# Filter halves on two load queues, a sign moved into a product, and a shifted schedule, in an FFT-mixing plus swish-MLP kernel

## The chip, the cores and the metric

The kernel runs on one core of a Trainium2 chip. The metric is the device time of one execution in microseconds (us). TensorE (PE in the profile) multiplies, VectorE (DVE), ScalarE (ACT) and GpSimd (POOL) do the rest, and loads are issued by SyncE (SP) and by GpSimd; they then run on 16 DMA engines.

## The reference, cut to what matters

```python
# x (8, 3008, 256); filt_r, filt_i (1505, 256); w_in (256, 2048); w_out (2048, 256)
X = np.fft.rfft(x, axis=1)
y = np.fft.irfft(X * (filt_r + 1j * filt_i), n=3008, axis=1)   # per batch and channel
h = y.reshape(24064, 256) @ w_in
out = (h / (1 + exp(-beta * h))) @ w_out
```

The transform of length 3008 = 47 x 64 is done in two stages as matrix products (s1 and s2 forward, s3 and s4 inverse). The filter is applied between s2 and s3.

## The kernel before

The program has two parts. The **setup** loads the filters and weights, builds the DFT tables and transforms batch 0, since no MLP can run before a batch is mixed. The **main loop** has 752 steps; each does one slice of the MLP (`hps`, silu to `gT`, `acc`), and a plan places pieces of the later batches' transforms between them.

```python
# setup: filters, 128 partitions; the upper 64 hold the same values as the lower 64
def load_filter(f_sb, filt, ks, ds):
    lo = AP(...)   # rows k0.. , 32 partitions
    hi = AP(...)   # mirrored rows, 32 partitions
    for p0, src in ((0, lo), (M, lo), (H, hi), (M + H, hi)):      # M = 64, H = 32
        nc.sync.dma_start(f_sb[p0 : p0 + H, ks, ds], src)
# called six times: fr, fi for the first 8 k; fr, fi for the rest, twice (two column halves)
...
def s2_0(n):                       # six units for batch 0
    ... matmuls into ps ...
    nc.vector.tensor_tensor(p_t[:], ps[:], fr_sb[:, ks, ds], ALU.mult)
    nc.vector.tensor_tensor(q_t[:], ps[:], fi_sb[:, ks, ds], ALU.mult)
...                                # s3_0 needs p_t, q_t and the tables t3, t3q
    nc.gpsimd.tensor_copy(t3q[:M, ks, :], t3[M:, ks, :])
    nc.gpsimd.tensor_scalar(t3q[M:, ks, :], t3[:M, ks, :], -1.0, None, ALU.mult)
...
wst = left.enter_context(tc.tile_pool(name="wstage", bufs=2))     # w_out staging
...
nc.gpsimd.tensor_copy(hold[:1], fr_sb[:1, NK - 1, D - 1 :])       # waits for the last fr
nc.gpsimd.dma_start(win_sb[:], ...)                               # w_in
for g in range(4):
    load_x(1, g)                                                  # two DMAs each, GpSimd
load_wout(0); load_wout(WG)                                       # SyncE, staged in wst
...
nc.gpsimd.tensor_scalar(t4[0:4], t4[0:4], 0.5, None, ALU.mult)    # table of s4
...
scale_wout(0); scale_wout(WG)      # GpSimd: wout_sb = ws / beta
for f0 in range(2 * WG, NFB, WG):
    load_wout(f0); scale_wout(f0)
...
left.close()                       # wst and others give their memory back
gpool = ...                        # gT of the main loop
```

Between the stages of the later batches the data go through DRAM: `a1_store` and `a2_load` around s1 and s2, a store of z and `zz_load` around s3 and s4.

Of the kernel before, what the change touches and what calls it, by code (L numbers as in the profile page):

```python
# [36 lines left out]
def kernel(  # L37
# [42 lines left out]
    def load_filter(f_sb, filt, ks, ds):  # L80
        k0, n, d0, w = ks.start, ks.stop - ks.start, ds.start, ds.stop - ds.start
        lo = AP(filt.tensor, filt.offset + k0 * D + d0, [[N1 * D, H], [D, n], [1, w]])
        hi = AP(filt.tensor, filt.offset + (N1 - k0) * D + d0, [[N1 * D, H], [-D, n], [1, w]])
        for p0, src in ((0, lo), (M, lo), (H, hi), (M + H, hi)):
            nc.sync.dma_start(f_sb[p0 : p0 + H, ks, ds], src)  # L85

    t1 = consts.tile([NP, KP], BF16, name="t1", tag="t1")
    t4 = consts.tile([KP, NP], BF16, name="t4", tag="t4")
    t2 = consts.tile([P, NK, P], BF16, name="t2", tag="t2")
    t3 = consts.tile([P, NK, P], BF16, name="t3", tag="t3")  # L90
    t3q = consts.tile([P, NK, P], BF16, name="t3q", tag="t3q")
    beta_sb = consts.tile([P, NFB], F32, name="beta_sb", tag="beta_sb")
    rbeta_sb = consts.tile([P, NFB], F32, name="rbeta_sb", tag="rbeta_sb")
    win_sb = wpool.tile([P, NDC, FF], BF16, name="win_sb", tag="win_sb")
# [31 lines left out]
    def small(name, dt=F32):  # L126
        return sp.tile([P, 1], dt, name=name, tag=name)
# [45 lines left out]
    iota(c4[:], [[0, NK], [1, 2], [0, 2]], base=1)  # L173
    iota(qq[:], [[0, NK], [0, 2], [1, 2]])
    make_identity(nc, ident)
    nc.gpsimd.tensor_copy(fr_sb[:1, 0, :1], x0[:1, 2 * MQ, :1])
    with nc.allow_non_contiguous_dma(reason="2048 values, once"):
        nc.sync.dma_start(beta_sb[:], moe_beta.rearrange("(fb fp) -> fp fb", fp=P))
    first, rest = slice(0, KH), slice(KH, NK)
    for ks, ds in ((first, slice(0, D)), (rest, slice(0, P)), (rest, slice(P, D))):  # L180
        load_filter(fr_sb, filt_r, ks, ds)
# [37 lines left out]
    def s1_0(g, on_act):  # L219
        ps = bank2([P, NDC, 512])  # L220
        for e in range(NDC):
            for i in range(MG):
                nc.tensor.matmul(
                    ps[:, e, i * 2 * NK : (i + 1) * 2 * NK],
                    lhsT=x0[:, g * MG + i, e * P : (e + 1) * P],
                    rhs=t1d[:],
                    start=True,
                    stop=True,
                )
        src = ps[:, :, : MG * 2 * NK].rearrange("p e (m k) -> p e k m", k=2 * NK)  # L230
        evac(aTv[:, g], src, on_act)
# [23 lines left out]
    s1_0(2, False)  # L255
    s1_0(3, True)
    t2_part(1, 1)
    keep = small("keep")
    kp2 = small("kp2")
    nc.vector.tensor_scalar(keep[:], ip[:], float(M), None, ALU.not_equal)  # L260
    nc.vector.tensor_scalar(kp2[:], ip[:], float(P - 1), None, ALU.not_equal)
    nc.vector.tensor_tensor(keep[:], keep[:], kp2[:], ALU.mult)
    n1s = small("n1s")
    q_p = small("q_p")
    n1_i = small("n1_i", I32)
# [2 lines left out]
    nc.vector.tensor_scalar(q_i[:], ip[:], 1, None, ALU.bitwise_and)  # L268
    nc.vector.tensor_scalar_mul(n1s[:], n1_i[:], TURN / N1)
    nc.vector.tensor_copy(q_p[:], q_i[:])  # L270
    kkf, c4f, qqf = (t[:].rearrange("p a b c -> p (a b c)") for t in (kk, c4, qq))
    nc.vector.tensor_scalar_mul(c4f, c4f, TURN / 4)
    nc.vector.scalar_tensor_tensor(kkf, kkf, n1s[:], c4f, ALU.mult, ALU.add)
    fold(kkf)
    sn = sq.tile([P, KP], F32, name="sn", tag="sn")
    nc.scalar.activation(sn[:], kkf, ACT.Sin, scale=TWO_PI / TURN)
    s1_0(4, False)
    s1_0(5, True)
    nc.vector.scalar_tensor_tensor(
        t1[:], qqf[:NP], q_p[:NP], sn[:NP], ALU.is_equal, ALU.mult  # L280
    )
    s1_0(6, False)
    s1_0(7, True)
    a0_turn(0, (False, True))
    r_sq.close()

    def t3_part(g):
        tp = bank2([P, 2 * KH, P], BF16)
        ks = slice(g * KH, (g + 1) * KH)
        for e in range(KH):  # L290
            nc.tensor.transpose(tp[:, e, :], t2[:, g * KH + e, :], ident[:])
        nc.scalar.activation(t3[:, ks, :], tp[:, :KH, :], ACT.Copy)
        if g == 0:
            nc.gpsimd.tensor_scalar(t3[:, 0, :], t3[:, 0, :], keep[:], None, ALU.mult)
        nc.gpsimd.tensor_copy(t3q[:M, ks, :], t3[M:, ks, :])
        nc.gpsimd.tensor_scalar(t3q[M:, ks, :], t3[:M, ks, :], -1.0, None, ALU.mult)

    t3_part(0)

    xpool = ctx.enter_context(tc.tile_pool(name="xpool", bufs=4))  # L300
    ypool = ctx.enter_context(tc.tile_pool(name="ypool", bufs=2))
# [74 lines left out]
    def s2_0(n):  # L376
        kg, e = units[n]
        ds = slice(e * P, (e + 1) * P)
        ps = bank2([P, KH, P])
        for kk_ in range(KH):  # L380
            k1 = kg * KH + kk_
            nc.tensor.matmul(
                ps[:, kk_, :], lhsT=t2[:, k1, :], rhs=a0[:, k1, ds], start=True, stop=True
            )
        ks = slice(kg * KH, (kg + 1) * KH)
        p_t = p0pool.tile([P, KH, P], BF16, name="p_t", tag="p_t")
        q_t = p0pool.tile([P, KH, P], BF16, name="q_t", tag="q_t")
        nc.vector.tensor_tensor(p_t[:], ps[:], fr_sb[:, ks, ds], ALU.mult)
        nc.vector.tensor_tensor(q_t[:], ps[:], fi_sb[:, ks, ds], ALU.mult)  # L389
        pq[n] = (p_t, q_t)  # L390

    def s3_0(n):
# [18 lines left out]

    units = [(0, 0), (0, 1), (1, 0), (2, 0), (1, 1), (2, 1)]
    s2_0(0)
    a0_turn(1, (True, True))
    t3_part(1)
    s2_0(1)
    s3_0(0)
# [105 lines left out]
    def s2(b, i, split):  # L523
        ps, ks = s2_matmuls(b, i)
        if split:
            p_t = yhpool.tile([P, 2, D], BF16, name="p_t", tag="p_t")
            q_t = yhpool.tile([P, 2, D], BF16, name="q_t", tag="q_t")
            nc.vector.tensor_tensor(p_t[:], ps[:], fr_sb[:, ks, :], ALU.mult)
            nc.vector.tensor_tensor(q_t[:], ps[:], fi_sb[:, ks, :], ALU.mult)
            st["yh", b, i] = ((t3, p_t), (t3q, q_t))  # L530
            return
        a_t = abpool.tile([P, 2, D], F32, name="a_t", tag="a_t")
        b_t = abpool.tile([P, 2, D], F32, name="b_t", tag="b_t")
        yh = yhpool.tile([P, 2, D], BF16, name="yh", tag="yh")
        nc.vector.tensor_tensor(a_t[:], ps[:], fr_sb[:, ks, :], ALU.mult)  # L535
        nc.vector.scalar_tensor_tensor(  # L536
            b_t[:M], ps[M:], -1.0, fi_sb[:M, ks, :], ALU.mult, ALU.mult
        )
        nc.vector.tensor_tensor(b_t[M:], ps[:M], fi_sb[:M, ks, :], ALU.mult)  # L539
        nc.gpsimd.tensor_tensor(yh[:], a_t[:], b_t[:], ALU.add)  # L540
        st["yh", b, i] = ((t3, yh),)
# [48 lines left out]
    def at(s, fn, *a):  # L590
        plan.setdefault(int(s), []).append((fn, a))

    def s1_steps(b, steps, act):
        assert len(steps) == J // 2
        for i, s in enumerate(steps):
            at(s, s1, b, i, act and i % 2 == 1)
            if i % 4 == 3:
                at(s, a1_store, b, i // 4)
# [7 lines left out]
    def s4_steps(b, steps, act):  # L606
        assert len(steps) == J // 4 * NDC
        for i, s in enumerate(steps):
            at(s, s4, b, i, act and i % 2 == 1)

    for b in range(1, B):
        o = first_step[b - 1]
        if b == 1:
            s1_steps(1, [o + 4 + i for i in range(16)], True)
            for g in range(NG):
                at(o + 23, a2_load, 1, g)
            base = [o + 30 + s for s in (0, 3, 6, 9, 12, 14, 20, 22, 24, 26, 28, 30)]
            s23_steps(1, base, 3, True)
            for h in range(J // JG):
                at(o + 67, zz_load, 1, h)  # L620
            s4_steps(1, [o + 71 + i // 2 for i in range(16)], True)
            if B > 2:
                for g in range(4):
                    at(o + 24 + 2 * g, load_x, 2, g)
                s1_steps(2, [o + 40 + 2 * i for i in range(16)], False)
                for g in range(NG):
                    at(o + 76, a2_load, 2, g)
                if B > 3:
                    for g in range(4):
                        at(o + 52 + 8 * g, load_x, 3, g)  # L630
            continue
        base = [o + 16 * n + s for n in range(4) for s in (4, 8, 12)]
        s23_steps(b, base, 6, False)
        for h in range(J // JG):
            at(o + 72, zz_load, b, h)
        s4_steps(b, [o + 78 + i for i in range(16)], False)
        if b + 1 < B:
            early = [o + 16 * n + s for n in range(4) for s in (7, 13)]
            late = [o + s for s in (66, 67, 69, 70, 72, 73, 75, 76)]
            s1_steps(b + 1, early + late, False)  # L640
            for g in range(NG):
                at(o + 82, a2_load, b + 1, g)
            if b + 2 < B:
                for g in range(4):
                    at(o + (30, 62, 72, 78)[g], load_x, b + 2, g)

    blk = {}
    LAG = 2
# [75 lines left out]
```

## Time and profile before

| | before |
|---|---|
| median of 3 runs | 823.14 us (822.07 to 823.37) |
| first MLP matmul | 64.4 us |
| first / last q_t starts | 24.05 / 54.65 us |
| last fi_sb row lands | about 52.4 us |
| TensorE's waits after 66 us | 9.8 us in all |

The page of the kernel before: its length, and the shares of the chain of work that ended last, followed back from the end (a q marks the queue that issues, so SPq is SyncE issuing loads; "issue" is time in which an engine waited for nothing that the profile shows).

```profile
span 821.0 us, 15283 instructions
...
PE 84%; DMA 9%; SPq 2%; DVE 1%; issue 1%; ACT 1%; POOL 0%; DVEq 0%; POOLq 0%; ACTq 0%
```

TensorE dominates the whole, but this is an average of two regimes. The chain of waits of the kernel before, from 30 to 60 us (start, us, what), shows the other one:

```profile
34.79 1.13 SPq L85
...
35.96 16.34 DMA fi_sb<-in_filt_i_dram
...
52.38 1.24 DVE q_t L389
```

SyncE issues filter loads (L85) until 36 us; the last of them takes 16.3 us to land, and the product q_t waits for it. Two of VectorE's lines of the timeline, the first q_t and the one that waits longest (in brackets: idle time before, and what ended it):

```profile
24.05 1.23 DVE L389 TENSOR_TENSOR q_t<-sps,fi_sb 128x1024 bf16<-128x1024 f32 x1 [1.18 <-DMA fi_sb<-in_filt_i_dram]
...
52.38 1.23 DVE L389 TENSOR_TENSOR q_t<-sps,fi_sb 128x1024 bf16<-128x1024 f32 x1 [12.49 <-DMA fi_sb<-in_filt_i_dram]
```

The windows view of the kernel before (the stretch and its length; busy time, and number of instructions, of TensorE, of its weight loads, of VectorE, ScalarE and GpSimd; then granted clock of TensorE, DMA share and GB/s) shows the rate of the loads:

```profile
15.00:20.00 5.00, 4.07 (x56) 3.92 (x57) 2.79 (x5) 1.79 (x3) 0.00 (x0) 1.00 1.04 226
20.00:25.00 5.00, 3.08 (x43) 2.58 (x40) 2.17 (x2) 4.46 (x5) 2.81 (x3) 1.00 1.17 227
25.00:30.00 5.00, 3.34 (x60) 3.44 (x61) 3.06 (x4) 2.52 (x4) 4.88 (x3) 1.00 1.22 222
30.00:35.00 5.00, 1.36 (x17) 0.82 (x13) 1.86 (x3) 2.63 (x4) 3.81 (x3) 0.99 1.22 220
```

The last number of each line, 220 to 227 GB/s, is a plateau, and no compute engine is busy all of that time: the setup is load-bound. Two GpSimd lines of the timeline and the first MLP matmul (start, us, engine, line, operation):

```profile
35.82 0.83 POOL L424 DMA_DIRECT2D win_sb<-in_moe_w_in_dram  x1
...
47.98 0.46 POOL L434 TENSOR_SCALAR t<-t 4x94 bf16<-4x94 bf16 x1
...
64.39 0.38 PE L659 MATMUL hps<-y,win_sb 128*128 128x512 bf16 x1 [0.31 <-ACT y L104]
```

In the main loop there is little to win. TensorE's waits from 66 us to the end (who waited for whom, us in total, times, longest):

```profile
PE ps L577 <- DMA zz<-d: 6.4, 5, 2.1
PE acc L679 <- DVE ost L690: 1.6, 2, 1.3
PE ps L514 <- DMA a<-d: 1.2, 1, 1.2
```

### The profile page before, as it was taken

What the parts mean: (1) busy time and instruction counts of PE and PEld (TensorE: products, weight loads), DVE (VectorE), ACT (ScalarE), POOL (GpSimd) and SP (SyncE); (2) the same over time, 40 slices, a digit from 0 to 9 for tenths busy, and PEclk for the clock granted to TensorE, in tenths of its full rate; (3) what the DMA queues carried; (4) which work ended last, traced back from release to release, by engine and by line L of the source; (5) the groups of instructions that cost most, each with busy time, mean ns of one, the idle gap of its engine ahead of it and who ended that gap; (6) DMA issues with size and microseconds to landing.
All of it is one profiled execution on the core that took longest, in us unless ns stands there. A gap on an engine that the chain in (4) does not pass through costs nothing.

```text
span 821.0 us, 15283 instructions
## 1 busy us (share of the span) xinstructions
PE 768.3 (94%) x6036; PEld 551.7 (67%) x6129; DVE 437.1 (53%) x683; ACT 554.0 (67%) x805; POOL 150.7 (18%) x167
## 2 busy tenths in 40 slices
PE   4649899899999999999999999999999999999997
PEld 4535566676667766686667766677667766676664
DVE  7523378367655666457655676557665556330101
ACT  3547655677666676677666767676766777777775
POOL 4823001023211212012220222102210122000000
PEclk9969999999999999999999999999999999999999
DMA  9984736813393145804176232931237021410101
GB/s 161 222 201 101 184 102 159 223 50 83 78 242 91 55 106 111 243 26 119 56 174 166 72 85 68 238 104 46 79 112 202 28 90 46 123 53 26 52 26 52
DMA packets 93144, 91.45 MB, mean 111 GB/s; under 512 B 6156, under 2 KB 84492, under 8 KB 92756
## 3 DMA queue, kind: packets, MB, share of 16 engines
q1 hardware_dynamic: 88896, 77.09, 32.3%
q0 software_dynamic: 4176, 13.37, 10.5%
q8 instruction: 48, 0.79, 0.4%
q14 instruction: 24, 0.20, 0.1%
HBM read 57.16 MB, written 46.66 MB: 126 GB/s over the span
## 4 chain that ended last, share of the span: by engine, by line
PE 84%; DMA 9%; SPq 2%; DVE 1%; issue 1%; ACT 1%; POOL 0%; DVEq 0%; POOLq 0%; ACTq 0%
PE acc L679 38%; PE hps L659 35%; DMA zz<-d 4%; PE ps L577 3%; PE ps L551 3%; PE ps L492 2%; PE ps L514 2%; SPq L85 2%; DMA fi_sb<-in_filt_i_dram 2%; DMA d<-z 2%; DMA fr_sb<-in_filt_r_dram 1%; DMA x<-in_x_dram 1%; DVE ost L690 0%; DMA a<-d 0%; DVE z L106 0%
## 5 line engine op out<-in xcount | busy, mean ns | idle before, releaser
L668 ACT ACTIVATE gT<-hps,beta_sb 128x512 bf16<-128x512 f32 x752 | 516.7, 687 | 225.5 <-PE hps L659 200.5
L679 PE MATMUL acc<-wout_sb,gT 128*128 128x256 bf16 x3008 | 454.3, 273 | 3.3 <-DVE ost L690 1.6
L659 PE MATMUL hps<-y,win_sb 128*128 128x512 bf16 (+7 forms) x1635 | 428.3, 350 | 1.3 <-DVE y L108 0.5
L679 PEld LDWEIGHTS <-gT 128*128 128x128 bf16 x3008 | 287.0, 98 | 125.9 <-issue 2.8
L659 PEld LDWEIGHTS <-win_sb 128*128 128x128 bf16 x1728 | 165.0, 98 | 26.1 <-issue 1.9
L540 POOL TENSOR_TENSOR yh<-a_t,b_t 128x512 bf16<-128x512 f32 x72 | 91.1, 1265 | 403.2 <-DVE b_t L539 396.6
L690 DVE COPY ost<-acc 128x512 f32<-128x512 f32 x94 | 60.4, 685 | 135.6 <-PE acc L679 135.6
L106 DVE CAST a<-ps 96x512 bf16<-96x512 f32 x104 | 70.8, 685 | 55.4 <-PE ps L492 49.3
L108 DVE TENSOR_SCALAR y<-ps 128x376 bf16<-128x376 f32 x104 | 57.1, 549 | 66.9 <-PE ps L577 66.8
L535 DVE TENSOR_TENSOR a_t<-ps,fr_sb 128x512 f32<-128x512 f32 x72 | 49.8, 692 | 69.1 <-PE ps L514 68.4
L106 DVE CAST z<-ps 128x512 bf16<-128x512 f32 x84 | 57.4, 684 | 7.9 <-PE ps L551 7.0
L577 PEld LDWEIGHTS <-zz 96*128 96x128 bf16 x448 | 30.4, 98 | 31.7 <-DMA zz<-d 7.9
L536 DVE SCALAR_TENSOR_TENSOR b_t<-ps,fi_sb 64x512 f32<-64x512 f32 x72 | 49.9, 692 | 1.0
L539 DVE TENSOR_TENSOR b_t<-ps,fi_sb 64x512 f32<-64x512 f32 x72 | 49.2, 683 | 1.0
L492 PE MATMUL ps<-xg,t 94*96 94x512 bf16 x112 | 42.7, 382 | 0.7
L577 PE MATMUL ps<-t,zz 96*128 96x94 bf16 x448 | 36.2, 206 | 7.6 <-DMA zz<-d 6.4
L312 POOL DMA_DIRECT2D xg<-in_x_dram x28 | 15.3, 545 | 114.2 <-PE ps L492 114.2
L514 PE MATMUL ps<-a,t 128*128 128x256 bf16 x168 | 32.1, 273 | 1.5 <-DMA a<-d 1.2
L551 PE MATMUL ps<-yh,t 128*128 128x256 bf16 x144 | 27.5, 273 | 0.5
L514 PEld LDWEIGHTS <-t 128*128 128x128 bf16 x168 | 16.1, 98 | 16.8 <-issue 1.5
L551 PEld LDWEIGHTS <-t 128*128 128x128 bf16 x168 | 16.2, 98 | 16.2
L401 PE MATMUL sps<-t3q,q_t 128*128 128x128 bf16 x48 | 8.7, 272 | 14.5 <-DVE q_t L389 12.6
(94 smaller groups left out, 236.7 us busy)
## 6 DMA issues: line engine op xcount, KB each, us to landing
out_dram<-ost SPq DMA_DIRECT2D x47, 512.0 KB, 3.0
d<-a SPq DMA_DIRECT2D x28, 384.0 KB, 5.1
a<-d SPq DMA_DIRECT2D x28, 384.0 KB, 5.2
d<-z SPq DMA_DIRECT2D x28, 384.0 KB, 4.0
zz<-d SPq DMA_DIRECT2D x28, 384.0 KB, 7.3
xg<-in_x_dram POOLq DMA_DIRECT2D x28, 320.0 KB, 5.9
fr_sb<-in_filt_r_dram SPq DMA_DIRECT2D x12, 256.0 KB, 7.5
fi_sb<-in_filt_i_dram SPq DMA_DIRECT2D x12, 256.0 KB, 7.5
```

Source lines behind the costliest of these rows:

```text
L106: nc.vector.tensor_copy(dst, src)
L108: nc.vector.tensor_scalar_mul(dst, src, scale)
L492: nc.tensor.matmul(ps[:KP], lhsT=t1[:], rhs=xg[b, g][:, jj : jj + 2, :], start=True, stop=True)
L514: nc.tensor.matmul(ps[:, e, :], lhsT=t2[:, k0 + e, :], rhs=st["a2", b, g][:, kk + e, :], start=True, stop=True,)
L536: nc.vector.scalar_tensor_tensor(b_t[:M], ps[M:], -1.0, fi_sb[:M, ks, :], ALU.mult, ALU.mult)
L540: nc.gpsimd.tensor_tensor(yh[:], a_t[:], b_t[:], ALU.add)
L551: nc.tensor.matmul(ps[:, e, :], lhsT=tab[:, 2 * i + e, :], rhs=src[:, e, :], start=n == 0, stop=n == len(srcs) - 1,)
L577: nc.tensor.matmul(ps[:, e, :NP], lhsT=zz[:, j0 % JG + e, dc * P : (dc + 1) * P], rhs=t4[:], start=True, stop=True,)
L659: nc.tensor.matmul(hps[:, pos - t0 : pos - t0 + ln], lhsT=win_sb[:, dc, fb * P : (fb + 1) * P], rhs=ys[b][:, dc, n0 : n0 + ln], start=(dc ...
L668: nc.scalar.activation(gT[:], hps[:], ACT.Silu, scale=beta_sb[:, fb : fb + 1])
L679: nc.tensor.matmul(acc[tb // 2][:, tb % 2, :], lhsT=gT[:, tb * P : (tb + 1) * P], rhs=wout_sb[:, fb, :], start=(fb == 0 and tb % 2 == 0), ...
L690: nc.vector.tensor_copy(ost[:, 2 * h : 2 * h + 2, :], acc[h][:])
```

## The change

Its intent: load the lower and upper 64 partitions of the filters through two queues at the same time; let the product q_t carry the sign of the inverse, so that GpSimd only copies t3q; and give the reads from DRAM (zz, a2) and the x loads other steps, so that TensorE no longer waits for them. Cut to its core:

```diff
-        for p0, src in ((0, lo), (M, lo), (H, hi), (M + H, hi)):
+        for p0, src in ((0, lo), (H, hi)):
             nc.sync.dma_start(f_sb[p0 : p0 + H, ks, ds], src)
+            nc.gpsimd.dma_start(f_sb[M + p0 : M + p0 + H, ks, ds], src)
...
-    nc.gpsimd.tensor_copy(fr_sb[:1, 0, :1], x0[:1, 2 * MQ, :1])
+    nc.sync.dma_start(seen[:], x0[:1, 2 * MQ, :2])        # SyncE starts after x0's third part
...                                      # first-DFT evictions ahead of small table work on VectorE
-            nc.gpsimd.tensor_scalar(t3[:, 0, :], t3[:, 0, :], keep[:], None, ALU.mult)
+    nc.vector.memset(t2[:, 0, M : P : M - 1], 0.0)        # in its place, before the transpose
-        nc.gpsimd.tensor_scalar(t3q[M:, ks, :], t3[:M, ks, :], -1.0, None, ALU.mult)
+        nc.gpsimd.tensor_copy(t3q[M:, ks, :], t3[:M, ks, :])
...
-        nc.vector.tensor_tensor(q_t[:], ps[:], fi_sb[:, ks, ds], ALU.mult)
+        nc.vector.scalar_tensor_tensor(
+            q_t[:], ps[:], sgn[:], fi_sb[:, ks, ds], ALU.mult, ALU.mult)
...                                      # plan, o = first step of the batch before
-            s1_steps(1, [o + 4 + i ...], True)            # and a2 at 23, s2 from 30, zz at 67
+            s1_steps(1, [o + 3 + i ...], False)           # and a2 at 20, s2 from 29, zz at 63
-                    at(o + 24 + 2 * g, load_x, 2, g)
-                s1_steps(2, [o + 40 + 2 * i ...], False)
-                    at(o + 76, a2_load, 2, g)
+                    at(o + 32 + 2 * g, load_x, 2, g)
+                s1_steps(2, [o + 46 + 2 * i ...], False)
+                    at(o + 82, a2_load, 2, g)
-            at(o + 72, zz_load, b, h);  s4_steps(b, [o + 78 + i ...])
+            at(o + 70, zz_load, b, h);  s4_steps(b, [o + 80 + (i * 13) // 15 ...])
-                    at(o + (30, 62, 72, 78)[g], load_x, b + 2, g)
+                    at(o + (30, 62, 88, 92)[g], load_x, b + 2, g)
```

## The prediction

> **What bounds the kernel now.** Two regimes. After about 66 us TensorE sets the pace: its waits view lists only 9.8 us there (6.4 for zz tiles, 1.6 for the output eviction, 1.2 for a2 tiles); about 6 us more is the drain at the end. Before that, the setup (first MLP matmul at 64.4 us in the timeline) is bound by the filter loads: the chain of waits runs from 11.6 to 36 us through SyncE issuing them, then 16.3 us through the last fi_sb load, landing at 52.4. VectorE waited 16.8 us for fi_sb, 12.5 of it once. The windows view shows 220 to 225 GB/s from 15 to 40 us, for 1 KB and 512 B rows alike. Every filter load fills 32 partitions; the Trainium skill, "SBUF — State Buffer", section "Door 1: The DMA port swizzle", gives about 218 GB/s as the asymptote there (8 of 16 ports); 222 agrees. Loads of all partitions reach 290 to 370 here (a2 and zz windows). After 36 us the last 1.6 MB of filters also share the engines with w_in, x and w_out.
>
> **What the change does.**
> 1. Lower and upper halves come by SyncE and GpSimd at once. The same page ("Can I just issue two DMAs to hit both halves?") says two such loads gained only 6%. I expect more here, 260 to 300 GB/s; estimate for 6.3 MB from 11 us: done at 32 to 36 us. Even at 6% half of the filters now stand ahead of w_in in GpSimd's queue: done by about 40 instead of 52.4.
> 2. GpSimd pays 12 issues: issues took 0.51 to 0.83 us; estimate 0.8 to 1.2 each for these shorter rows, 12 us, ending near 23. Its negations of t3q (2.76 us x3) become copies (1.03), and the 0.62 keep goes. The first s3 product, waiting for t3q until 26.66, stays near 25 to 27.
> 3. VectorE's q_t carries the sign: scalar_tensor_tensor of 64x512 took 692 ns against 683 for the plain product: free.
> 4. Earlier evictions of the first DFT: about 1 us.
>
> **Critical path.** With filters in time, products 2 to 5 follow the first s3 by about 12 us (8 x 1.22 plus 2.8), ending near 40 instead of 55.9; from there to the first MLP matmul took 8.5. First MLP matmul: 47 to 52, say 49: 15 us saved. Main loop: zz loads get 10 steps of room instead of 6, and x loads no longer fall on them or on batch 1's a2: 5 of the 9.2 us go, and the half-clock stretch after the 147 us stall (3.4 us at 0.5) gives 1.5 more. Batch 2's first DFT ends 6 steps later, leaving 8 steps before its a2 is wanted: maybe 1 us back. Net 6.
>
> **Predicted: 802 us**, 8 in 10 within 795 to 811. Faster by over 2% (under 806.7) 0.70, within 2% 0.29, slower 0.01.
>
> **Right or wrong by:** last fi_sb landing before 41 us; over 245 GB/s between 15 and 30 us; GpSimd's filter issues over by 25 us; first MLP matmul between 46 and 53; TensorE's waits for zz under 1.5 us, for a2 under 2; no half-clock stretch near 147 us.
>
> **What would make it wrong:** GpSimd issues of 512 short rows costing 2 us or more, or held behind earlier loads (the trace shows one issue held 7.1 us until w_in landed), delaying t3q and all behind it: then 808 to 812. Or w_in landing becomes the new last wait.

## The result

The changed kernel takes 819.6 us (median of 3, 819.31 to 820.23) against 823.14. The ratio is 0.9962 with a 95% interval of 0.9939 to 0.9984; here and below it is the mean time of one kernel's fast runs over that of the other's of the same rounds, so not quite the ratio of the medians. The change is a little faster, far from the predicted 802 us and outside its range.

| | before | after |
|---|---|---|
| first q_t starts | 24.05 | 29.68 |
| last q_t starts | 54.65 | 46.66 |
| w_in issued | 35.8 | 40.0 |
| first MLP matmul | 64.39 | 62.10 |
| from there to the last output eviction | 750.8 | 749.6 |

The last row is 815.22 minus 64.39 and 811.74 minus 62.10. So of 3.5 us, the setup gave 2.3 (predicted: 15) and the main loop 1.2 (predicted: 6).

The page of the changed kernel:

```profile
span 817.3 us, 15269 instructions
...
PE 87%; DMA 2%; DVE 2%; issue 1%; ACT 0%; DVEq 0%; SPq 0%; ACTq 0%
```

This chain says nothing of the setup: the profile follows it back only to 62.9 us (its shares add up to 92%, those of before to 98%). What the setup waits for now has to be read from its stages. The windows view of the changed kernel, in the same stretches:

```profile
15.00:20.00 5.00, 4.10 (x55) 3.77 (x52) 3.45 (x12) 1.83 (x4) 2.87 (x5) 1.00 1.03 240
20.00:25.00 5.00, 2.18 (x37) 1.99 (x35) 1.22 (x1) 1.53 (x2) 2.72 (x3) 1.00 1.04 262
25.00:30.00 5.00, 0.00 (x0) 0.00 (x0) 0.32 (x1) 0.00 (x0) 0.00 (x0) 0.65 1.07 241
30.00:35.00 5.00, 3.98 (x38) 3.98 (x39) 3.89 (x4) 3.20 (x4) 1.36 (x2) 0.50 1.18 212
```

More bytes move until 30 us (240 to 262), fewer afterwards (212). And from 25 to 30 us nearly everything stands still: TensorE does nothing at all. During that stall its clock was halved, from 26.5 to 36.7 us by the clock records (0.65 and 0.50 above, 0.83 from 35 to 40 us); in the kernel before the clock stayed full until 34.9. VectorE's lines of the timeline say why; the first is the first q_t, the second the last fi_sb that it had to wait for:

```profile
29.68 1.28 DVE L388 SCALAR_TENSOR_TENSOR q_t<-sps,sgn,fi_sb 128x1024 bf16<-128x1024 f32 x1 [4.78 <-DMA fi_sb<-in_filt_i_dram]
...
44.33 1.28 DVE L388 SCALAR_TENSOR_TENSOR q_t<-sps,sgn,fi_sb 128x1024 bf16<-128x1024 f32 x1 [1.58 <-DMA fi_sb<-in_filt_i_dram]
```

The last fi_sb comes 8 us sooner than before, but the first comes 5.6 us later. The DMA view of the changed kernel from 24 to 30 us (queue, packets, MB, share; q0 is GpSimd's queue, q1 SyncE's) shows who was served:

```profile
q0 software_dynamic: 383, 1.25, 86.6%
q1 hardware_dynamic: 383, 0.22, 19.8%
```

The packet counts are equal and the bytes are not. GpSimd's packets hold 3.3 KB on average (1.25 MB over 383), SyncE's 0.57 KB. The Trainium skill, "DMA: Bandwidth & Descriptors", section "Queues, rings and completion order", says that each DMA engine takes turns between queues packet by packet; this trace agrees, 383 to 383, and nearly so in each 2 us from 20 to 30 us (113 to 111, 124 to 120, 134 to 131, 119 to 119, 130 to 133). A product needs both halves of its filter, so it got the pace of SyncE's 35 to 40 GB/s (0.22 MB in 6 us).

After the last q_t (46.66) the first MLP matmul takes another 15.4 us (before: 9.7). GpSimd's lines of the timeline, with TensorE's first MLP matmul:

```profile
39.99 0.75 POOL L425 DMA_DIRECT2D win_sb<-in_moe_w_in_dram  x1
...
51.89 0.52 POOL L312 DMA_DIRECT2D xg<-in_x_dram  x1 [7.43 <-DMA win_sb<-in_moe_w_in_dram]
52.43 0.48 POOL L435 TENSOR_SCALAR t<-t 4x94 bf16<-4x94 bf16 x1
...
62.10 0.38 PE L662 MATMUL hps<-y,win_sb 128*128 128x512 bf16 x1 [0.34 <-DVE y L110]
```

The eighth x load is held until w_in has landed. In the compiled program GpSimd's loads signal eight completion semaphores in turn, and this load, the eighth after w_in, first waits on the one that w_in signals. The halving of the table t4 (L435) stands behind it in GpSimd's queue. This was so before as well, at 47.4 and 48.0 us, but then the last filters were later still. Now it is TensorE's last long wait of the setup, in its waits up to 70 us:

```profile
PE sps L356 <- POOL t L435: 6.2, 1, 6.2
```

In the main loop the zz wait is gone, and another has grown. TensorE's waits of the changed kernel after 60 us begin with:

```profile
PE ps L515 <- DMA a<-d: 5.4, 2, 3.7
```

The longer of the two, 3.7 us, is batch 2's a2 at 157 to 160.8 us. The windows around it, where the third number from the right is the granted clock:

```profile
157.00:160.00 3.00, 0.09 (x3) 0.00 (x0) 0.00 (x0) 0.69 (x2) 0.00 (x0) 0.94 1.03 299
160.00:167.00 7.00, 6.21 (x31) 3.75 (x31) 2.27 (x4) 1.78 (x3) 2.30 (x3) 0.54 0.81 181
```

TensorE stood still from 157.1 to 160.8 us, and its clock was halved for 6.8 us, from 159.6, still within the wait, to 166.5 (clock records); 5.7 us of that were work. Before, there was one such stretch of 3.4 us (147.6 to 151.0), after the zz wait that began at 145 us:

```profile
147.00:151.00 4.00, 3.56 (x26) 2.63 (x28) 1.10 (x2) 1.55 (x3) 0.00 (x0) 0.57 1.05 244
```

From the first MLP matmul to the last output eviction TensorE's idle time fell from 14.9 to 11.8 us and its busy time grew from 736.0 to 737.9: 3.1 - 1.9 = 1.2, the measured gain. Of the 1.9, the longer work at half clock explains about 1.1 (half of 5.7 less half of 3.4); the rest was not traced.

### The profile page after: what moved, and what is told of

Its sections match the earlier page's. It is cut to its first block, busy times and chain, and to the rows that moved or that the text cites. A ratio compares the mean times of both kernels' runs of the same rounds, so it can differ in the third digit from the quotient of the medians.

```text
span 817.3 us, 15269 instructions
## 1 busy us (share of the span) xinstructions
PE 770.1 (94%) x6037; PEld 552.8 (68%) x6129; DVE 442.4 (54%) x691; ACT 550.0 (67%) x796; POOL 152.8 (19%) x177
## 3 DMA queue, kind: packets, MB, share of 16 engines
HBM read 57.16 MB, written 46.66 MB: 127 GB/s over the span
## 4 chain that ended last, share of the span: by engine, by line
PE 87%; DMA 2%; DVE 2%; issue 1%; ACT 0%; DVEq 0%; SPq 0%; ACTq 0%
PE acc L682 40%; PE hps L662 36%; PE ps L493 3%; PE ps L554 3%; PE ps L580 3%; PE ps L515 2%; DMA d<-a 1%; DMA a<-d 1%; DVE ost L693 1%; DVE a L108 1%; DVE q_t L530 0%; DVE p_t L529 0%; ACT gT L671 0%; DVE z L108 0%; DVEq L722 0%
## 5 line engine op out<-in xcount | busy, mean ns | idle before, releaser
L108 DVE CAST a<-ps 96x512 bf16<-96x512 f32 x112 | 76.0, 684 | 53.3 <-PE ps L493 47.3
L580 PE MATMUL ps<-t,zz 96*128 96x94 bf16 x448 | 33.9, 205 | 0.7
L493 PEld LDWEIGHTS <-t 94*96 94x96 bf16 x112 | 13.8, 124 | 10.5
```

What stands on the lines that cost most here:

```text
L108: nc.vector.tensor_copy(dst, src)
L493: nc.tensor.matmul(ps[:KP], lhsT=t1[:], rhs=xg[b, g][:, jj : jj + 2, :], start=True, stop=True)
L580: nc.tensor.matmul(ps[:, e, :NP], lhsT=zz[:, j0 % JG + e, dc * P : (dc + 1) * P], rhs=t4[:], start=True, stop=True,)
```

## The experiments

Theories for the setup: (A) the split starves SyncE's halves, because packets are taken in turn and GpSimd's are larger, and what it gains at the end is masked by t4's halving; against it, (B) SyncE's loads or the lower partitions are slow for a reason of their own, or w_in, w_out or total bytes set the end. For the main loop: (C) batch 2's first DFT is now too late for its a2; against it, contention of stores and x loads. All experiments are edits of the changed kernel; all gave correct results. The runs came in four groups (e1 to e4; e1b, e5 to e7; e9 to e11; e12), each on a chip of its own, with the kernel before at 822.3, 823.6, 824.0 and 824.5 us (medians) beside them; so across groups the ratios are compared. The columns of us are read from the one profiled execution of each run.

| run | first q_t | last q_t | first MLP matmul | first silu | time | ratio to before (95%) |
|---|---|---|---|---|---|---|
| before | 24.05 | 54.65 | 64.39 | 65.73 | 823.1 | 1 |
| changed | 29.68 | 46.66 | 62.10 | 63.43 | 819.6 | 0.9962 (0.9939 to 0.9984) |
| e1b: t4 on VectorE | 30.98 | 47.01 | 57.34 | 62.74 | 820.0 | 0.9947 (0.9922 to 0.9972) |
| e2: one queue | 24.01 | 56.13 | 65.89 | 67.44 | 823.7 | 1.0003 (0.9959 to 1.0047) |
| e3: queues exchanged | 30.03 | 46.95 | 63.05 | 64.38 | 819.5 | one look |
| e4: batch 2's steps | 28.75 | 46.06 | 62.23 | 63.77 | 812.9 | 0.9891 (0.9867 to 0.9915) |
| e6: one queue, hold | 24.08 | 46.10 | 55.31 | 64.07 | 815.1 | 0.9897 (0.9868 to 0.9926) |
| e7: e1 and e4 | 31.40 | 47.15 | 58.96 | 62.49 | 813.1 | 0.9864 (0.9835 to 0.9892) |
| e9: one queue, order | 24.78 | 46.73 | 59.32 | 60.44 | 811.0 | 0.9843 (0.9819 to 0.9867) |
| e11: split, order | 29.70 | 46.62 | 59.05 | 60.17 | 809.9 | 0.9827 (0.9800 to 0.9855) |
| e10: half the bytes | 23.39 | 43.21 | 56.13 | 57.45 | 805.8 | 0.9781 (0.9757 to 0.9804) |
| e12: e10 mended | 22.54 | 40.49 | 53.38 | 54.72 | 803.9 | 0.9759 (0.9715 to 0.9804) |

### e1 and e1b: t4's halving on VectorE

```diff
-    nc.gpsimd.tensor_scalar(t4[0:4], t4[0:4], 0.5, None, ALU.mult)
+    nc.vector.tensor_scalar(t4[0:4], t4[0:4], 0.5, None, ALU.mult)
```

> The changed kernel with one line altered: the halving of t4's first four rows runs on VectorE instead of GpSimd, where it stood behind the eighth x load, which is held until w_in has landed at 51.9 us. Theory (the halving is the last wait of the setup): TensorE's 6.2 us wait for t4 goes, the first MLP matmul moves from 62.1 to about 56.5 us, the whole to about 814 us. Rival (the setup now ends with the landing of w_in or of the x and w_out loads themselves): the first MLP matmul stays within 1 us of 62.1 and the time near 819.6.

The profiled execution took 2,094 us, with every TensorE matmul at about twice its usual duration, so its profile is of no use; the other three took 818.8 to 820.9 us. The kernel was run again:

> The same kernel as the first experiment, because its profile fell in an execution of 2,094 us whose matmuls took over twice as long all through, while its three other times (818.8 to 820.9) showed no gain. Theory as before: first MLP matmul near 56.5 us. If the time stays near 820 while the first MLP matmul comes early, the gain is given back in batch 1 and must show as longer TensorE waits for a2, or as half-clock stretches, after 62 us. Rival: the first MLP matmul itself stays near 62 us, held by something else.

It took 820.0 us, and the profile shows that both the theory and its failure are true. From e1b's timeline:

```profile
57.34 0.38 PE L662 MATMUL hps<-y,win_sb 128*128 128x512 bf16 x1 [0.34 <-DVE y L110]
...
60.82 3.74 POOL L324 TENSOR_TENSOR wout_sb<-ws,rbeta_sb 128x1024 bf16<-128x1024 f32 x2 [4.36 <-DMA ws<-in_moe_w_out_dram]
62.74 1.26 ACT L671 ACTIVATE gT<-hps,beta_sb 128x512 bf16<-128x512 f32 x2 [5.49 <-POOL wout_sb L324]
```

The first MLP matmul came 4.8 us earlier, as expected, and then the first silu waited 5.5 us for GpSimd's scaling of w_out's third piece. The silu reads nothing of that piece. The compiled program of e1b, built again from its kernel, gives the reason: gT's first buffer has the address of the staging buffer that held the third piece, and the first silu waits on GpSimd's semaphore for that piece's scaling. That piece was loaded late because its load waits for a staging buffer, hence for GpSimd's first scaling, which again stands behind the held x load (52.7 us), and then shares the engines with the x loads. In the changed kernel the first silu ran at 63.43, only 1 us after the same scaling allowed it (60.56 + 1.9 = 62.5). So two waits lay one behind the other, and removing one alone gained nothing.

### e2: the filters back on one queue

```diff
-        for p0, src in ((0, lo), (H, hi)):
+        for p0, src in ((0, lo), (M, lo), (H, hi), (M + H, hi)):
             nc.sync.dma_start(f_sb[p0 : p0 + H, ks, ds], src)
-            nc.gpsimd.dma_start(f_sb[M + p0 : M + p0 + H, ks, ds], src)
```

> The changed kernel with the filter loads back on SyncE alone, in the order of before; all else as changed. Theory (the split starves SyncE's halves, so that the first fi half lands about 5 us later than before, and only half of the late landing is repaired): the first q_t goes back from 29.7 to about 24 us, the last fi_sb lands at 47 to 52 instead of 44.3, w_in is issued near 34 instead of 40, and the first MLP matmul comes at 59 to 63, within 2.5 us of the changed kernel: the split as it stands is worth almost nothing. Rival (the split is worth the 8 us by which the last fi_sb lands earlier, and something else in the change costs time): first MLP matmul at 66 or later, total 825 or more.

First q_t at 24.0, first MLP matmul at 65.9, 823.7 us. The last fi_sb was even later than expected, as VectorE's line in e2's timeline shows:

```profile
53.80 1.28 DVE L387 SCALAR_TENSOR_TENSOR q_t<-sps,sgn,fi_sb 128x1024 bf16<-128x1024 f32 x1 [13.78 <-DMA fi_sb<-in_filt_i_dram]
```

The first q_t came back to 24 us, as theory A says. The first MLP matmul moved by 3.8 us, more than the 2.5 expected and just short of the rival's 66. So the split as it stands is worth about 4 us in the setup of these profiles (in the times 0.4%, with intervals that overlap); e6 and e11 tell through what.

### e3: the two queues exchanged

```diff
-            nc.sync.dma_start(f_sb[p0 : p0 + H, ks, ds], src)
-            nc.gpsimd.dma_start(f_sb[M + p0 : M + p0 + H, ks, ds], src)
+            nc.gpsimd.dma_start(f_sb[p0 : p0 + H, ks, ds], src)
+            nc.sync.dma_start(f_sb[M + p0 : M + p0 + H, ks, ds], src)
```

> The changed kernel with the two queues exchanged: SyncE loads partitions 64 to 127, GpSimd 0 to 63. Theory (the engines take packets from the two queues in turn, and GpSimd's packets are about six times as large as SyncE's 512 bytes): SyncE's queue starves again, with equal packet counts and under 50 GB/s against about 200 while both have work; the first q_t again waits for a SyncE load, near 29 to 30 us. Rival (the lower partitions or their addresses are the slow ones): now GpSimd's loads land late, and SyncE's move at 150 GB/s or more beside them.

The DMA view of e3 from 24 to 30 us:

```profile
q0 software_dynamic: 379, 1.24, 86.5%
q1 hardware_dynamic: 381, 0.21, 19.1%
```

SyncE starves again, now with the upper partitions, and the first q_t is at 30.0. The rival of slow partitions or addresses falls.

### e4: batch 2's first DFT at the steps of before

```diff
-                s1_steps(2, [o + 46 + 2 * i for i in range(16)], False)
-                    at(o + 82, a2_load, 2, g)
+                s1_steps(2, [o + 40 + 2 * i for i in range(16)], False)
+                    at(o + 76, a2_load, 2, g)
```

> The changed kernel with batch 2's first DFT at the steps of before (46+2i back to 40+2i) and its a2 loads at 76 instead of 82. Theory (the later steps cost 3.7 us of TensorE waiting at 156 us and, through it, 6.8 us at half clock): the wait for a2 near 156 us and the half-clock stretch after it vanish, the total falls by 5 to 7 us to about 813 to 815. Rival (the wait is made by the stores' and x loads' contention, not by the step): a wait of 2 us or more stays there and the total falls by less than 2 us.

812.9 us: 6.6 us less than the one look at e3 on the same chip, which behaves like the changed kernel, or 0.7% (5.8 us) by the ratios. TensorE's waits of e4 after 100 us are a single line:

```profile
PE acc L682 <- DVE ost L693: 0.5, 1, 0.5
```

The a2 wait and the half-clock stretch after it are gone: theory C holds. The two together (3.7 us, and half of the 5.7 us worked at half clock) add up to about 6.5. In e3, whose main loop is that of the changed kernel, the wait was 4.0 us and the stretch only 3.4, so its length differs between executions.

### e5: the upper halves on ScalarE's queue

```diff
-            nc.gpsimd.dma_start(f_sb[M + p0 : M + p0 + H, ks, ds], src)
+            nc.scalar.dma_start(f_sb[M + p0 : M + p0 + H, ks, ds], src)
```

> The changed kernel with the upper filter halves issued from ScalarE's queue instead of GpSimd's: both queues then send packets of one row each. A look at the loads, not a better kernel, since ScalarE's issues stand among its evictions. Theory (packets in turn): the two queues move about equal bytes, each 110 to 130 GB/s, together 225 to 260, and no half lands much after its partner. Rival (SyncE's loads are slow for a reason of their own, such as their later start): SyncE stays under 60 GB/s while the other queue has work.

827.4 us: ScalarE was held up by its own issues and the first DFT ran late. From 24 to 30 us ScalarE's queue moved 0.65 MB and SyncE's 0.72, together 228 GB/s, so SyncE's loads are not slow by themselves when their rival sends single rows. But SyncE's queue moved almost nothing from 16 to 20 us, for a reason that I did not find, and packet counts were not equal (1315 to 531, SyncE's being longer rows of the first part). It supports theory A without proving the turn-taking a second time.

### e6: one queue, w_in held until the last filter

```diff
 (e2, e1 and e4, and)
-    nc.gpsimd.tensor_copy(hold[:1], fr_sb[:1, NK - 1, D - 1 :])
+    nc.gpsimd.tensor_copy(hold[M + H :][:1], fi_sb[M + H : M + H + 1, NK - 1, D - 1 :])
```

> A version meant to beat both: the changed kernel with the filters back on SyncE alone, w_in and the x loads held until the last fi_sb row is in (instead of the last fr_sb row of partition 0), t4 halved on VectorE, batch 2 at the steps of before. Theory (what made the last filters late before was w_in's and x's large packets): the last fi_sb lands near 40 us, w_in near 47, first MLP matmul near 52, total 802 to 806. Rival (the setup is bound by total bytes to be moved, in whatever order): first MLP matmul at 58 or later, total 809 or more.

From e6's timeline, VectorE's last wait for fi_sb, and the first silu:

```profile
43.77 1.28 DVE L387 SCALAR_TENSOR_TENSOR q_t<-sps,sgn,fi_sb 128x1024 bf16<-128x1024 f32 x1 [3.73 <-DMA fi_sb<-in_filt_i_dram]
...
64.07 1.26 ACT L670 ACTIVATE gT<-hps,beta_sb 128x512 bf16<-128x512 f32 x2 [8.84 <-POOL wout_sb L323]
```

One queue, left alone, has its last fi_sb in at 43.8 us: the split's 44.3 is no better. What had made it 52 to 54 was the company of w_in and x. The first MLP matmul came at 55.3 (expected 52), but the same scaling of w_out cost 8.8 us, so the time was 815.1 and not 802 to 806. The miss is the mechanism of e1b, not yet known when this was sent.

### e7: the split with both repairs

It has the edits of e1 and of e4.

> The changed kernel with the two one-line repairs together, t4 halved on VectorE and batch 2 at the steps of before; the split stays. If the repairs add: first MLP matmul near 56.5 us and 806 to 809 in all. If t4 is worth nothing, as the first experiment's times suggest: 812 to 814, as with batch 2's steps alone.

813.1 us, as e4 alone (812.9): t4's repair is worth nothing while the silu waits for w_out (first silu 62.5).

### e9 and e11: the later loads in another order

Both have the repairs of e7. In e9 the filters come by SyncE alone, in e11 by the split.

```diff
-    wst = left.enter_context(tc.tile_pool(name="wstage", bufs=2))
+    wst = left.enter_context(tc.tile_pool(name="wstage", bufs=4))
 (1/beta computed on VectorE at about 17 us instead of after the last q_t)
-    nc.gpsimd.tensor_copy(hold[:1], fr_sb[:1, NK - 1, D - 1 :])
+    for f0 in range(0, NFB, WG):
+        load_wout(f0)
+    for f0 in range(0, 3 * WG, WG):
+        scale_wout(f0)
     nc.gpsimd.dma_start(win_sb[:], ...)
-    for g in range(4):
+    load_x(1, 0)
+    scale_wout(3 * WG)
+    for g in range(1, 4):
         load_x(1, g)
```

> One queue for the filters, and the order of the later loads mended: all four w_out pieces staged at once (4 buffers instead of 2) and loaded ahead of w_in, 1/beta computed early, GpSimd scales three w_out pieces before it issues w_in, and the fourth before the second of the four x loads; t4 halved on VectorE, batch 2 at the steps of before. Theory (in the t4 and hold experiments the first silu stood behind the scaling of w_out's third piece, whose load was starved by w_in and x packets): the 4.5 to 7.2 us that TensorE lost right after the first MLP matmul go; first MLP matmul near 55.5 us, first silu within 2 us of it, total 806 to 809. Rival (the silu waits for something else): the stall after the first MLP matmul stays above 4 us, total 813 or more.

> The same order of the later loads and the same repairs, but the filters split over SyncE and GpSimd as in the change. Theory (the split moves no more bytes per us over the whole of the filters, since one queue alone runs at about 200 once the other is done; it only delays the first half-pairs): last fi_sb at 42 to 45 us as with one queue, first q_t at 29 to 31 instead of 24, first MLP matmul 0 to 3 us later than in the one-queue run, total 807 to 811. Rival (the split is worth its 8 us once nothing else masks it): first MLP matmul before 52 us, total under 804.

The stall after the first MLP matmul is gone (first silu 1.1 us after it in both). In the compiled program of e9, with four buffers, the first silu waits for the scaling of the first piece and no longer of the third. The first MLP matmul itself was later than expected, 59.3 and 59.05, because this order issues w_in only at 51 us; e9's timeline shows it waiting:

```profile
59.32 2.87 PE L658 MATMUL hps<-y,win_sb 128*128 128x512 bf16 x6 [3.16 <-DMA win_sb<-in_moe_w_in_dram]
```

So both missed part of the gain, and the first MLP matmul cannot tell the two apart. The last q_t can: 46.73 with one queue, 46.62 with two. And so can the bytes. The windows view from 14 to 40 us, the time in which the filters load, first of the kernel before:

```profile
14.00:40.00 26.00, 16.17 (x217) 14.90 (x217) 14.36 (x21) 14.06 (x17) 16.43 (x18) 0.93 1.17 224
```

Then of the changed kernel:

```profile
14.00:40.00 26.00, 14.43 (x181) 13.66 (x182) 12.42 (x21) 11.24 (x14) 10.99 (x18) 0.80 1.11 230
```

Of e9, one queue:

```profile
14.00:40.00 26.00, 15.95 (x218) 14.48 (x217) 15.28 (x28) 13.04 (x16) 6.39 (x8) 0.93 1.15 226
```

And of e11, the split:

```profile
14.00:40.00 26.00, 14.21 (x173) 13.50 (x174) 12.57 (x26) 11.22 (x14) 10.93 (x15) 0.80 1.11 226
```

224, 230, 226, 226 GB/s: over the whole of the filters, two queues move no more than one. What they gain while both run (240 to 262) they lose once GpSimd's queue is empty: from 32 to 38 us of the changed kernel SyncE alone, now filling partitions 0 to 63 only, moved 201 GB/s (e3, with partitions 64 to 127: 202), where the queue of before, going to and fro between the two halves, moved 222 (25 to 30 us).

### e10 and e12: half of the bytes

The upper 64 partitions hold the same values as the lower 64. e10 is e9 with only the lower half loaded and the upper copied on the chip.

```diff
+    def copy_up(f_sb, n, on_act):   # f_sb[M:, ks, ds] <- f_sb[:M, ks, ds]
+    ...                             # fi and fr's first part on GpSimd, fr's rest on ScalarE
```

> As the one-queue order run, but only partitions 0 to 63 of the filters are loaded; the upper 64, which hold the same values, are copied from them on GpSimd (fi, and fr's first part) and ScalarE (fr's rest). Theory (the setup is bound by the bytes of the filter loads at about 222 GB/s): 3.1 MB instead of 6.3, last filter row near 28 us, first MLP matmul at 46 to 50, total 799 to 804. Rival (with the loads out of the way the chain of transposes and products is as long): first MLP matmul later than 53, total 805 or more.

805.8 us. The first MLP matmul, 56.1 us, misses the theory's 46 to 50 and is later than the rival's 53; the total lies just above the theory's range. One queue that fills only partitions 0 to 63 moved 194 GB/s from 14 to 27 us (199 in e12) and not the 222 that I had assumed, and the last fi half was in at about 32.9 us instead of 28. Nor were bytes the only bound. Part of it was my own: VectorE's line of e10 for t4's halving shows a wait of 4.5 us before it, with the next products behind it, since ScalarE's eviction of t4 came late.

```profile
36.12 0.90 DVE L457 TENSOR_SCALAR t<-t 4x94 bf16<-4x94 bf16 x1 [4.49 <-ACT t L456]
```

e12 mends that and issues w_in before w_out's scalings:

```diff
-    nc.vector.tensor_scalar(t4[0:4], t4[0:4], 0.5, None, ALU.mult)
+    nc.scalar.activation(t4[0:4], tp4[0:4, 0, :NP], ACT.Copy, scale=0.5)
 (w_in and the first x load issued ahead of the four scale_wout)
```

> The run with half of the filter bytes, with two of its own new waits mended: in it VectorE stood 4.5 us before t4's halving, which now goes to ScalarE with t4's eviction, and w_in was issued only after three scalings of w_out, at 42.7 us; it is now issued before them. If those two waits were what kept the first MLP matmul at 56.1 us: 50 to 53 us now, total 799 to 803. If the chain of transposes, products and evictions at half clock is what remains: 54 to 56, total 803 to 806.

```profile
53.38 0.38 PE L671 MATMUL hps<-y,win_sb 128*128 128x512 bf16 x1 [0.31 <-ACT y L105]
```

803.9 us, ratio 0.9759 (0.9715 to 0.9804): about 2.4% faster than before, with an interval that reaches to just under 2%, and the lowest median. The first MLP matmul is at 53.4, a little beyond the expected 50 to 53; just before it stands a wait of 0.31 us for an eviction, where e9's stood 3.16 us for w_in. The last q_t starts at 40.5, so 12.9 us of evictions, transposes and products after it remain.

## Why the prediction was wrong, point by point

- *"What bounds the kernel now"* was right: filter loads in the setup, TensorE after it. e10 supports the first half: against e9 it changes only the filters' loads and the copies in their place, and its first MLP matmul came 3.2 us sooner and its time is about 5 us less. That 222 GB/s fell together with the figure for half of the ports carries little weight, though: the queue of before fed both halves in turn, and one half alone got 194 to 202.
- *Step 1, "I expect more here, 260 to 300 GB/s ... done at 32 to 36 us"*, failed. The rate check as put ("over 245 GB/s between 15 and 30 us") would just have passed (240, 262, 241: mean 248), but over all of the filters it was 230 against 224 before. I had looked at the rate of two queues while both run, and not at what remains when the faster is done. The skill's page, "SBUF — State Buffer", section "Can I just issue two DMAs to hit both halves?", had 6% for it, and was nearer to the mark than I was.
- *The last fi_sb "done by about 40 instead of 52.4"* came at 44.3. Its mechanism, no longer competing with w_in and x, was right; e6 gets the same (43.8) with one queue.
- *Step 2, "the first s3 product ... stays near 25 to 27"*, failed. GpSimd's issues were over at 22.8 us, as the sum of 23 had it, but by luck: they took only 0.65 us each, and the last three stood 4.3 us in all until earlier filter loads had landed. What failed was the wait: q_t stood until 29.7 for SyncE's starved half. I had added the two queues' rates and not asked how the engines divide themselves between them, and a product needs both halves.
- *"From there to the first MLP matmul took 8.5"*, counted from the end of the last q_t, failed: 14.2 us (47.9 to 62.1). I knew of the issue held until w_in lands, and feared for t3q, but did not look at what else stands behind it in GpSimd's queue: t4's halving, and then w_out's scalings, which e1b showed to be a second wait right behind the first.
- *Setup, 15 us saved*: 2.3. With one queue, batch 2's steps and the order mended, e9 has its first silu 5.3 us before the kernel before (60.44 against 65.73), e11, the split with the same order, 5.6, and e12 11.0; no run here came to 15, with the split or without.
- *Step 3*, the sign free of charge, held nearly: q_t of 128x1024 took 1.28 us instead of 1.23, six times. *Step 4*, earlier evictions of about 1 us, was not isolated.
- *Main loop, zz*: right, 6.4 us of waits became none.
- *"Batch 2's first DFT ends 6 steps later ... maybe 1 us back"*: the right mechanism, mis-sized. It was a wait of 3.7 us and 5.7 us of work at half clock, together about 6 us by e4. The half-clock stretch that I expected to vanish came back at another place, twice as long in the profiled execution (in e3 as long as before).
- *"x loads no longer fall on ... batch 1's a2"*: the shift of batch 2's x loads by 8 steps did nothing. GpSimd issued them at 69 to 83 us, at 73 to 87 before: as soon as s1 freed a buffer, since GpSimd has nothing else to do there and does not wait for the step.

Left open: by what the rate of one-sided loads is limited (I changed no port or partition layout), and how much of the end of the silu's wait in e9 is due to each of four buffers, the early 1/beta and the other order, which came together.

## What to carry to other kernels

In these traces SyncE's and GpSimd's queues shared the DMA engines by packets (383 each, for 0.22 and 1.25 MB), so the queue with small packets starved beside the one with large packets. Before splitting a load, ask which consumers need both parts, and measure the bytes over the whole transfer and not in the overlap. When a change takes away the last wait of a stage, list what else stands in the same in-order queue behind the same event, because a chain of waits hidden behind the first one can return all of the gain (t4, then w_out's scalings). Where loads bound a stage, fewer bytes (e10, e12) did more than another way to move the same bytes.

## What the Trainium skill lacked or had wrong

- "DMA: Bandwidth & Descriptors", "Queues, rings and completion order": turns by packet agree for SyncE beside GpSimd (383 to 383 and 379 to 381 packets); for ScalarE beside SyncE in e5 the counts were unequal (1315 to 531). It lacks the consequence: GpSimd's queue got 1.25 MB and SyncE's 0.22 MB of the same kind of load. The sentence under "Issuing engines are not separate DMA queues", that a second engine only saves issue time, leaves out that it also shifts the shares.
- "SBUF — State Buffer", "Can I just issue two DMAs to hit both halves?": +6% there; here 6 to 15% while both queues ran (240, 262 and 241 GB/s against 226, 227 and 222), and 0 to 3% over the whole (e11 against e9, 226 both; changed against before, 230 to 224). It does not say that a single queue which alternates between the halves already moves more (222) than one that fills one half (194 to 202).
- "TensorE: Matmul & The Clock Gate", "Part 1: The HAM clock gate", has one idle window of about 3.4 us before half clock, in windows that run freely. The stretches agree, being multiples of 3.4 us (3.4 and 6.8), but less idle time was enough: the clock was halved 2.5 us into the 3.7 us wait (157.1 to 159.6), and after a gap of only about 2 us (145.1 to 147.2) in the kernel before, while gaps of 1.7 us (changed kernel) and 2.2 us (e11) at batch 1's a2 were not followed by half clock.
- No page has a whole execution like e1's of 2,094 us: the `hps` matmuls took 753 ns on average where the changed kernel's took 351, and ScalarE's silu its usual 687 ns. Its trace holds no clock record, so the clock of 1.0 in its views says nothing. It did not come back in this kernel's seven other executions.
